# Sizes and pitches of shared on-chip buffers in a gated mix of linear attention and a dense layer

## The chip, the cores and the metric

The kernel runs on one core of one Trainium2 chip. The metric is device time in microseconds (us), the median of three runs. Beside it stands one profiled execution, with the start and duration of every instruction on TensorE (PE; its weight loads are PEld), VectorE (DVE), ScalarE (ACT), GpSimd (POOL) and SyncE (SP, which issues the DMAs).

## The reference

For x of 2048 rows and 640 columns:

```python
g = sigmoid((x * gate_w).sum(-1, keepdims=True))
q, k, v = split(x @ wqkv)                  # 32 heads of 20
phi(t) = concat([softmax(t @ w_phi), softmax(-(t @ w_phi))])   # per head, 40 features
kv = einsum("bhsf,bhsd->bhfd", phi(k), v)  # summed over all rows
z  = einsum("bhsf->bhf", phi(k))
a  = (phi(q) @ kv) / (phi(q) @ z + 1e-6) @ wo
b  = silu(x @ w1) @ w2                     # 1728 hidden columns
out = g * a + (1 - g) * b
```

All of it is float32. The kernel keeps the accuracy by splitting each operand of a matmul into a high part (rounded to float32r) and a low part (the rest), and by three matmuls for one product: high x high, high x low and low x high (PASSES).

## The kernel before, in words

The work has three stages, and TensorE is busy in all of them.

1. **Keys and values** (to about 172 us). The weights for keys and values are prepared in SBUF as two wide tiles, wh (high) and wl (low), of five row chunks with 1282 columns (WC): 640 key columns, 640 value columns and the gate with a column of zeros. For each of 16 tiles of 128 rows, kv_proj (line 470, and line 328 for the first two tiles) multiplies x (stationary, 128 x 128) by wh and wl (moving) in three column cuts: 0 to 500, 500 to 1000, 1000 to 1282. VectorE and ScalarE make the key features from it, v_part (lines 281 to 290) copies the values with high and low part into one of three value tiles vs (line 274), and kv_acc and kv_rest (lines 440 and 451) accumulate kv, with a value row as stationary and the key features as moving operand.

2. **Dense layer** (172 to about 580 us). For four blocks of 512 rows, h_parts (line 518) multiplies a piece of w1 (stationary) by x (moving, 512 elements), ScalarE applies SiLU, the result is split into u, and out_acc (line 706) multiplies a piece of w2 (stationary) by u (moving, 512 elements). One piece costs 15 matmuls at line 518 and 15 at line 706. For the first four pieces of the first block line 535 (h_first) takes the place of line 518. The weights stay in SBUF for all four blocks, in three places that load_f (line 251) chooses by order: the first NPRE = 9 in the pool fq (tiles w), the next ten in the two big buffers (tiles f), the rest in the pool fp (tiles w too). In the last block the fused query weights are made (lines 231 and 246) and the first query tiles run beside the dense work.

3. **Queries and output** (to the end). For eight blocks of 256 rows q_proj (line 429) multiplies x (stationary) by the query weights WQ (moving, 320 elements), VectorE, ScalarE and GpSimd make the features, TensorE transposes them (line 991), multiplies them by kv (line 1128) and by the output weights WO (line 1171; stationary, with oT as moving operand). The last rows of the output weights lie in a tile of their own, wor_s.

The order of work around the change is set in three ways: inside `with inorder(...)` the listed engines run in the order of the code (stage 1's start, the last dense block, and stage 3), a planner orders the rest, and SP issues all DMAs from one queue.

The change touches how SBUF is laid out. **Two big buffers** (tag "big", line 105) are used one after another for three things each: the first for wh, then the held weights f1, then WO; the second for wl, then f0, then WQ. A big buffer holds 2 x 5 x 642 float32r elements (25680 bytes a partition). As `big` it is seen as five chunks with a high and a low half of 642 elements, of which 640 are used; all high halves come first, then all low halves. As `big_kv` it is seen as five rows of 1282 elements without a gap. **The value tiles** (line 274) have 11 rows of 122 elements (VW): 60 high, 60 low, and two ones. The allocation of the pools pads each tile to a multiple of 32 bytes, and tiles of a pool follow each other, so the size of the big buffers decides where everything behind them begins: the raw tiles, the x slots, the pools fq and fu, and the pools that are opened in turn behind these (ta with the value tiles, then fp, then tb).

Of the kernel before, what the change touches and what calls it, by code (L numbers as in the profile page):

```python
# [9 lines left out]
F32R = mybir.dt.float32r  # L10
# [6 lines left out]
P = 128  # L17
S = 2048
D = 640
# [3 lines left out]
NC = D // P  # L23
# [7 lines left out]
GW = GR * DH  # L31
# [7 lines left out]
KG = -(-H // KH)  # L39
VW = KF + 2  # L40
# [10 lines left out]
EB = 2  # L51
KXB = 1
WC = 2 * D + 2
CUTS = (0, 500, 1000, WC)
RW = 114
NEARLY = 3
# [4 lines left out]
def mix_kernel(ctx: ExitStack, tc: tile.TileContext, xT, wqT, wkc, wkr, wv, bd, bdc, cst, wo, w1, w1r, w2, out):  # L61
# [3 lines left out]
    wp = ctx.enter_context(tc.tile_pool(name="wp", bufs=1))  # L65
# [3 lines left out]
    def opened(name, **kw):  # L69
        open_pools[name] = tc.tile_pool(name=name, bufs=1, **kw)  # L70
        return open_pools[name].__enter__()
# [7 lines left out]
    ta = opened("ta")  # L79
# [18 lines left out]
    def raw(name):  # L98
        return wp.tile([P, D + 2], F32, tag="raw", name=name, bufs=4)
# [2 lines left out]
        return (pool or wp).tile([P, 2, 512], F32R, tag=tag, name=name, bufs=bufs)  # L102

    def big_tile(name):
        return wp.tile([P, 2, NC, D + 2], F32R, tag="big", name=name, bufs=2)

    def big(name):
        return big_tile(name).rearrange("p s c d -> p c s d")

    def big_kv(name):  # L110

        return big_tile(name).rearrange("p s c d -> p (s c d)")[:, : NC * WC].rearrange("p (c w) -> p c w", w=WC)

    def wslot(name, dt=F32):
        return fq.tile([P, 2 * D], dt, tag="w", name=name, bufs=NPRE)

    def split(hi, lo, src, lo_eng="dve"):
        nc.scalar.copy(hi, src)  # L118
        eng = nc.vector if lo_eng == "dve" else nc.gpsimd
        eng.tensor_tensor(lo, src, hi.bitcast(F32), op=ALU.subtract)  # L120
# [130 lines left out]
    held = {}  # L251

    def load_f(n):
        w, f = seq[n]
        k = n - NPRE
        if 0 <= k < 10:
            if k % 5 == 0:
                held[k // 5] = big(f"f{k // 5}")
            t = held[k // 5][:, k % 5, :, :D]
        else:  # L260
            t = wslot(f"w{w}_{f}", F32R).rearrange("p (s d) -> p s d", s=2) if n < NPRE else fp.tile([P, 2, D], F32R, name=f"w{w}_{f}")
        r = raw(f"wr{w}_{f}")
        src = w1[f] if w == 1 else w2[f * P : (f + 1) * P, :]
        nc.sync.dma_start(r[:, :D], src)
        split(t[:, 0, :], t[:, 1, :], r[:, :D], "pool" if n < NPRE else "dve")
        W[w, f] = t

    def kv_cols(t, lo, hi):

        k = next(k for k in range(3) if CUTS[k] <= lo and hi <= CUTS[k + 1])  # L270
        return (kvp1 if t == 1 else kvp)[k][:, lo - CUTS[k] : hi - CUTS[k]]

    VB = 3
    vs = [ta.tile([P, KG, VW], F32R, name=f"v{k}") for k in range(VB)]
    for v in vs:
        nc.vector.tensor_copy(v[:, :, KF:], onesf[:, : KG * 2].rearrange("p (g f) -> p g f", f=2))
        nc.vector.tensor_copy(v[:, KG - 1, :KF], onesf[:, :KF])
# [14 lines left out]
    def flat(name):  # L292
        return ta.tile([P, D + 2], F32, tag="kx", name=name, bufs=KXB)

    warm = ps.tile([P, 512], F32, tag="pwk1", name="warm", bufs=1)
    for k in range(WARM):
# [6 lines left out]
        )  # L303

    WKV = [big_kv("wh"), big_kv("wl")]
    wh, wl = (w[:, :, :D] for w in WKV)
    LAST = D - NG * GW
# [33 lines left out]
    def v_weights(c):  # L341
        r = ta.tile([P, 2 * D], F32, tag="e", name="wvr1", bufs=EB)[:, : D + 2] if c == 1 else flat(f"wvr{c}") if c == 2 else raw(f"wvr{c}")
        nc.sync.dma_start(r, wv[c * P : (c + 1) * P, :])
        split(WKV[0][:, c, D:], WKV[1][:, c, D:], r)

    def values(t):
        return [(t, D, CUTS[2]), (t, CUTS[2], WC)]

    def keys(t):
        return [(t, 0, CUTS[1]), (t, CUTS[1], D)]  # L350

    def share(c, cols, opens=()):
        kv_share(c, [(*p, p in opens) for p in cols])

    with inorder(PE, ACT, DVE, POOL):
# [5 lines left out]
        nc.sync.dma_start(strest[: wkr.shape[0], :], wkr)  # L361
        for lo, hi in ((D, CUTS[2]), (CUTS[2], WC)):
            split(WKV[0][:, 0, lo:hi], WKV[1][:, 0, lo:hi], wv0[:, lo - D : hi - D])
# [12 lines left out]
        for c in range(NC):  # L376
            if c + 1 < NC:
                next(x0)
                v_weights(c + 1)
                nc.sync.dma_start(st0[c + 1], wkc[c + 1])  # L380
            for half in range(2):
                k_split_w(c, half, k_weights(c, half))
            if c == 0:
                share(1, values(0) + values(1))
            elif c < 3:
                share(c - 1, keys(0), keys(0)[:1] if c == 1 else ())
            else:
                share(c - 1, [(0, lo, hi) for lo, hi in zip(CUTS, CUTS[1:])])
        share(NC - 1, [(0, lo, hi) for lo, hi in zip(CUTS, CUTS[1:])])
# [198 lines left out]
    with inorder(ACT, DVE, POOL):  # L588
        for t in range(NT - 1):
# [29 lines left out]
            if t % 2 == 1:  # L619
                load_f(t // 2)  # L620
            if t + 2 == NT:
                for _ in range(4):
                    next(xf0)
                load_f(NPRE - 1)
        t = NT - 1
# [84 lines left out]
    with tc.issue_after(last["silu"].ins):  # L710
        for n in range(NPRE, len(seq)):
            load_f(n)
    r = raw("w1rr")
# [4 lines left out]
    r = raw("w2rr")  # L718
# [12 lines left out]

    def wo_split(c):
        r = wor_raw.pop(c)
        split(WO[:GW, c, 0, :D], WO[:GW, c, 1, :D], r[:GW, :D])

    def stack(dst, src, hi, col, n=GW):

# [149 lines left out]
    def make_kvw():  # L887

        parts = [w.rearrange("p j f -> p (j f)").rearrange("p (i q f) -> p i q f", q=4, f=KD) for w in kvw]
        for h in range(2):  # L890
            nc.gpsimd.memset(parts[h][:, :, 1:3].bitcast(F32), 0.0)  # L891
        pts = []
        for j0, n in ((0, 8), (8, 3)):
            pt = bank(f"pkvt{j0}")
            pts.append((j0, n, pt))
            for j in range(j0, j0 + n):
                w = min(KF, 2 * D - j * KF)
                nc.tensor.transpose(
                    pt[:w, (j - j0) * KD : (j - j0 + 1) * KD], kvb["kvm"][:, j * KF : j * KF + w], ident[:KD, :KD]
                )  # L900
        yield
        for j0, n, pt in pts:
            n = min(n, 2 * NG - j0)
            i0, i1 = j0 // 2, (j0 + n) // 2
            split(
                *(part[:, i0:i1, ::3] for part in parts),
                pt[:GW, : n * KD].rearrange("p (i a f) -> p i a f", a=2, f=KD),
            )
        split(
            *(kvwr[:, h].rearrange("p (k f) -> p k f", f=REST) for h in range(2)),  # L910
            pt[:RC, None, n * KD : n * KD + REST].to_broadcast([RC, KH, REST]),
        )
        yield
# [102 lines left out]
    with inorder(PE, DVE, ACT, POOL):  # L1016
# [3 lines left out]
        load_fused(0)  # L1020
        last_dense(4)
        WQ = big("wq")
        zbc = wslot("zbc")
        nc.sync.dma_start(zbc, kv_d[KF].partition_broadcast(P))

        def fuse(gi):
            return fused(kvb["bd"], WQ[:, :, 0, :], WQ[:, :, 1, :], gi)
# [7 lines left out]
        last_dense(6, fuse(1))  # L1035
        kvl_sum(1)
        WO = big("wo")
        load_fused(3)
        wo_load(0)
        last_dense(7, fuse(2))  # L1040
        wo_split(0)
        load_fused(4)
        wo_load(1)
        wo_load(2)
        last_dense(8, fuse(3))
        wo_split(1)
        wo_split(2)
        load_fused(5)
        wo_load(3)
# [3 lines left out]
        w = make_kvw()  # L1053
        last_dense(9, w)
        w = fuse(4)
# [7 lines left out]
        t = 2 * NP - 4  # L1063
# [395 lines left out]
```

## Time and profile before

| | us |
|---|---|
| median of three runs | 761.03 |
| lowest and highest run | 760.9, 761.24 |
| span of the profiled execution | 759.8 |
| PE busy | 755.0 |
| PEld busy | 664.9 |
| DVE busy | 371.6 |
| ACT busy | 266.4 |
| POOL busy | 264.3 |

The span reaches from the first to the last instruction of the profiled execution; that execution has no other time of its own in the profile. In a row of the groups by line stand line, engine, operation, the tiles (output <- inputs), the shapes, the count after an x, then busy us and the mean ns of one, then the idle time before. In a row of the timeline stand start, length, engine, line, operation, tiles, shape and count. In a row of one tile or line stand the shortest, median and longest duration in ns, and the first and last start. In a row of the waits stand who waited for whom, the us in total, how often, and the longest.

### The profile page before, as it was taken

The numbers are of one execution on the slowest core, as the hardware profiler recorded it, in microseconds if no ns is written. First come the engines' busy times: TensorE is split into PE (matmuls) and PEld (weight loads), VectorE is DVE, ScalarE is ACT, GpSimd is POOL, SyncE is SP. The second block draws the span as 40 slices with busy tenths as digits, with TensorE's granted clock in tenths as the row PEclk, the third lists the DMA queues.
The fourth block names the chain that finished last, engine by engine and source line by source line (L and its number), as shares of the span: only waits on it lengthen the run. The fifth ranks groups of instructions, "written<-read, shape, count | busy, mean of one in ns | idle before, by whom it ended". The sixth has DMA issues, their size and how long they took to land.

```text
span 759.8 us, 10642 instructions
## 1 busy us (share of the span) xinstructions
PE 755.0 (99%) x4249; PEld 664.9 (88%) x4249; DVE 371.6 (49%) x664; ACT 266.4 (35%) x483; POOL 264.3 (35%) x165
## 2 busy tenths in 40 slices
PE   9999999999999999999999999999999999999998
PEld 8888888888888888888888888888999999999998
DVE  4676666676641221112211122134578888787861
ACT  5444444337541311122111222224354443334341
POOL 2388777768000000000000000000356766855551
PEclk9999999999999999999999999999999999999999
DMA  7111111112650220002200014022003332111222
GB/s 254 54 53 53 53 53 53 60 49 83 206 175 1 69 83 1 1 0 72 84 0 1 1 40 154 8 81 85 6 29 127 97 104 70 54 52 43 70 70 91
DMA packets 35259, 50.17 MB, mean 66 GB/s; under 512 B 3541, under 2 KB 22885, under 8 KB 35210
## 3 DMA queue, kind: packets, MB, share of 16 engines
q1 hardware_dynamic: 35210, 49.50, 20.7%
q8 instruction: 33, 0.54, 0.3%
q14 instruction: 16, 0.13, 0.1%
HBM read 38.37 MB, written 11.11 MB: 65 GB/s over the span
## 4 chain that ended last, share of the span: by engine, by line
PE 97%; DVE 1%; DMA 0%; POOL 0%; ACT 0%; issue 0%; SPq 0%; POOLq 0%; DVEq 0%; ACTq 0%
PE acc L706 25%; PE ph L518 23%; PE kvp L470 16%; PE pq L429 9%; PE pa L1171 9%; PE pn L1128 4%; PE kv L440 2%; PE pT L991 2%; PE kvp L535 2%; PE kvp L328 1%; PE kvq L328 1%; PE pwk L317 1%; PE pwq L231 1%; DMA wvr<-wv 0%; POOL eq L840 0%; PE kvp L451 0%
## 5 line engine op out<-in xcount | busy, mean ns | idle before, releaser
L120 DVE TENSOR_TENSOR u<-ph,u 128x512 fp32r<-128x512 f32 x48 | 33.2, 692 | 188.5 <-ACT u L118 188.5
L706 PE MATMUL acc<-u,w 128*128 128x512 f32 x480 | 114.2, 391 | 0.0
L891 POOL MEMSET kvw<- 120x600 f32 x2 | 1.2, 598 | 321.1 <-PE ph L518 321.1
L706 PEld LDWEIGHTS acc<-u,w 128*128 128x128 f32 x480 | 89.7, 188 | 19.2
L518 PE MATMUL ph<-xf,w 128*128 128x512 f32 x420 | 99.7, 390 | 0.0
L521 ACT ACTIVATE ph<-ph 128x512 f32<-128x512 f32 x48 | 27.9, 582 | 192.6 <-PE ph L518 192.6
L518 PEld LDWEIGHTS ph<-xf,w 128*128 128x128 f32 x420 | 78.7, 188 | 16.6
L470 PE MATMUL kvp<-wh,xa 128*128 128x500 f32 (+1 forms) x420 | 93.0, 357 | 0.0
L470 PEld LDWEIGHTS kvp<-wh,xa 128*128 128x128 f32 x420 | 71.4, 188 | 9.9
L1171 PE MATMUL pa<-oT,wo 120*128 120x256 f32 x600 | 76.8, 282 | 0.0
L1171 PEld LDWEIGHTS pa<-oT,wo 120*128 120x128 f32 x600 | 73.7, 188 | 0.0
L706 PE MATMUL acc<-u,f 128*128 128x512 f32 x300 | 73.0, 394 | 0.0
L518 PE MATMUL ph<-xf,f 128*128 128x512 f32 x300 | 72.7, 394 | 0.0
L518 PEld LDWEIGHTS ph<-xf,f 128*128 128x128 f32 x300 | 56.4, 188 | 13.1
L706 PEld LDWEIGHTS acc<-u,f 128*128 128x128 f32 x300 | 56.1, 188 | 12.8
L804 POOL TENSOR_TENSOR ez<-eq,zbc 128x1280 f32<-128x1280 f32 x16 | 48.1, 3005 | 41.3 <-ACT eq L787 41.2
L120 POOL TENSOR_TENSOR ph<-ek,ph 128x1280 fp32r<-128x1280 f32 x16 | 47.4, 2964 | 26.8 <-ACT ph L118 26.8
L429 PE MATMUL pq<-wq,xb 128*128 128x320 f32 x360 | 55.5, 311 | 0.0
L429 PEld LDWEIGHTS pq<-wq,xb 128*128 128x128 f32 x360 | 53.0, 188 | 0.0
L470 PE MATMUL kvp<-wl,xa 128*128 128x500 f32 (+1 forms) x210 | 47.4, 356 | 0.0
L840 POOL TENSOR_TENSOR eq<-eq,sm 128x1280 f32<-128x1280 f32 x16 | 37.9, 2368 | 15.1 <-DVE sm L834 13.9
L498 POOL TENSOR_TENSOR ek<-ek,st 128x1280 f32<-128x1280 f32 x16 | 38.0, 2376 | 9.2 <-issue 6.1
(161 smaller groups left out, 1121.8 us busy)
## 6 DMA issues: line engine op xcount, KB each, us to landing
wr<-w SPq DMA_DIRECT2D x26, 320.0 KB, 3.9
xrf<-xT SPq DMA_DIRECT2D x20, 256.0 KB, 3.8
fb_d<-o SPq DMA_DIRECT2D x20, 256.0 KB, 2.4
y<-fb_d SPq DMA_DIRECT2D x16, 256.0 KB, 2.9
out<-y SPq DMA_DIRECT2D x16, 256.0 KB, 2.1
xra<-xT SPq DMA_DIRECT2D x14, 256.0 KB, 3.1
xrb<-xT SPq DMA_DIRECT2D x12, 256.0 KB, 2.7
wvr<-wv SPq DMA_DIRECT2D x5, 321.0 KB, 5.2
```

The costliest lines, as they stand in the source:

```text
L120: eng.tensor_tensor(lo, src, hi.bitcast(F32), op=ALU.subtract)
L328: nc.tensor.matmul(kv_cols(t, lo, hi), x_of(t)[c][:, hx, :], WKV[hw][:, c, lo:hi], start=(opens and hx == 0 and hw == 0), stop=(c == NC - ...
L429: nc.tensor.matmul(dst, xt[c][:, hx, :], w[:, c, hw, lo : lo + n], start=first, stop=(hx == 1 and c == NC - 1))
L470: nc.tensor.matmul(kv_cols(t, lo, hi), xt[c][:, hx, :], WKV[hw][:, c, lo:hi], start=(n == 0), stop=(n == 3 * NC - 1), skip_group_check=True,)
L498: nc.gpsimd.tensor_tensor(groups(e), groups(e), spread(st[:, 1, :]), op=ALU.mult)
L518: nc.tensor.matmul(ph, lhs, rhs, start=(n == 0), stop=(n == len(todo) - 1))
L521: nc.scalar.activation(hs, ph, AF.Silu)
L706: nc.tensor.matmul(acc[m], lhs, rhs, start=(f == order[0] and n == 0), stop=(f == order[-1] and n == len(todo) - 1))
L804: nc.gpsimd.tensor_tensor(ez, Q[t]["e"], zbc, op=ALU.mult)
L840: nc.gpsimd.tensor_tensor(groups(q["e"]), groups(q["e"]), spread(q["sm"][:, 2 * H : 4 * H]), op=ALU.mult)
L1128: nc.tensor.matmul(pns[u, gp][:GW, a, :], kvw_of(hk, 2 * i + jj)[:w], f[:w, hp, jj * 256 : (jj + 1) * 256], start=(n == 0), stop=(n == 3 * ...
L1171: nc.tensor.matmul(pa[:, a, :], WO[:GW, c, hw, ds] if c < NG else WOR[:, ds], o[:, ho, c, :], start=(k == 0), stop=(k == len(todo) - 1),)
```

## The change

Nothing of what is computed changes. The big buffer becomes a plain row of BIG = 2 x 5 x 640 + 32 = 6432 elements (25728 bytes). Seen as `big`, its chunks now hold high and low half next to each other, 640 elements each, without gaps. Seen as `big_kv`, a row has WS = 1284 elements of which 1282 are used. The value tiles get rows of 128 elements of which 122 are used. The remaining lines follow from that: slices that cut 642 down to 640 fall away, and a slice that ran to the end of a key and value row ends at WC.

```diff
 WC = 2 * D + 2
+WS = WC + 2
+BIG = 2 * NC * D + 32
...
     def big_tile(name):
-        return wp.tile([P, 2, NC, D + 2], F32R, tag="big", name=name, bufs=2)
+        return wp.tile([P, BIG], F32R, tag="big", name=name, bufs=2)
 
     def big(name):
-        return big_tile(name).rearrange("p s c d -> p c s d")
+        return big_tile(name)[:, : 2 * NC * D].rearrange("p (c s d) -> p c s d", c=NC, s=2)
 
     def big_kv(name):
 
-        return big_tile(name).rearrange("p s c d -> p (s c d)")[:, : NC * WC].rearrange("p (c w) -> p c w", w=WC)
+        return big_tile(name)[:, : NC * WS].rearrange("p (c w) -> p c w", w=WS)
...
-            t = held[k // 5][:, k % 5, :, :D]
+            t = held[k // 5][:, k % 5]
...
-    vs = [ta.tile([P, KG, VW], F32R, name=f"v{k}") for k in range(VB)]
+    vs = [ta.tile([P, KG, P], F32R, name=f"v{k}")[:, :, :VW] for k in range(VB)]
...
-        split(WKV[0][:, c, D:], WKV[1][:, c, D:], r)
+        split(WKV[0][:, c, D:WC], WKV[1][:, c, D:WC], r)
...
-        split(WO[:GW, c, 0, :D], WO[:GW, c, 1, :D], r[:GW, :D])
+        split(WO[:GW, c, 0], WO[:GW, c, 1], r[:GW, :D])
```

## Prediction

> **What bounds the kernel now.** I read the head of the page first, then the chain that ended last, then the waits of TensorE.
>
> ```profile
> span 759.8 us, 10642 instructions
> PE 755.0 (99%) x4249; PEld 664.9 (88%) x4249; DVE 371.6 (49%) x664; ACT 266.4 (35%) x483; POOL 264.3 (35%) x165
> PEclk9999999999999999999999999999999999999999
> PE 97%; DVE 1%; DMA 0%; POOL 0%; ACT 0%; issue 0%; SPq 0%; POOLq 0%; DVEq 0%; ACTq 0%
> ```
>
> ```profile
> PE warm L297 <- DVE ones L158: 1.1, 1, 1.1
> PE kvp L328 <- ACT wh L118: 0.2, 1, 0.2
> PE pT L991 <- POOL eq L840: 0.2, 1, 0.2
> ```
>
> TensorE is busy 755.0 of 759.8 us, 97% of the chain lies on it, its clock is granted in full in every slice, and all that it waited for another engine comes to 1.5 us. So the end moves only if matmuls themselves follow each other faster or slower. An edit that shortens work of another engine gives nothing here. The question is therefore the pace of the matmul stream: the time from the start of one matmul to the start of the next. The duration of a single row is longer than that, since matmuls overlap; the timeline shows the pace as the distance between the starts of two blocks, over the matmuls in the block.
>
> The dense part has one shape throughout (128 rows, 128 columns, 512 moving elements), and stationary tiles in three places: w tiles in the pool fq, w tiles in the pool fp, and f tiles, which are the ten weights held in the two big buffers. That makes it a control experiment inside the trace. First fq, then the big buffers, then fp, all from the timeline of TensorE:
>
> ```profile
> 282.75 3.56 PE L518 MATMUL ph<-xf,w 128*128 128x512 f32 x15
> 286.15 3.56 PE L706 MATMUL acc<-u,w 128*128 128x512 f32 x15
> 289.55 3.56 PE L518 MATMUL ph<-xf,w 128*128 128x512 f32 x15
> 292.95 3.56 PE L706 MATMUL acc<-u,w 128*128 128x512 f32 x15
> 296.35 3.59 PE L518 MATMUL ph<-xf,f 128*128 128x512 f32 x15
> ```
>
> ```profile
> 216.14 3.62 PE L518 MATMUL ph<-xf,f 128*128 128x512 f32 x15
> 219.60 3.64 PE L706 MATMUL acc<-u,f 128*128 128x512 f32 x15
> 223.07 3.66 PE L518 MATMUL ph<-xf,f 128*128 128x512 f32 x15
> 226.57 3.66 PE L706 MATMUL acc<-u,f 128*128 128x512 f32 x15
> 230.06 2.46 PE L518 MATMUL ph<-xf,w_r 128*128 128x512 f32 x10
> ```
>
> ```profile
> 342.54 3.60 PE L518 MATMUL ph<-xf,w 128*128 128x512 f32 x15
> 345.97 3.60 PE L706 MATMUL acc<-u,w 128*128 128x512 f32 x15
> 349.41 0.85 PE L518 MATMUL ph<-xf,w 128*128 128x512 f32 x3
> ```
>
> Sixty matmuls from fq take 296.35 - 282.75 = 13.60 us, or 3.40 us a block of 15 (226.7 ns a matmul). Sixty from the big buffers take 230.06 - 216.14 = 13.92 us, or 3.48 us a block (232.0 ns). Thirty from fp take 349.41 - 342.54 = 6.87 us, or 3.435 us a block (229.0 ns). Nothing but the place of the stationary operand differs. The groups by line say the same of all matmuls, with a smaller size:
>
> ```profile
> L706 PE MATMUL acc<-u,w 128*128 128x512 f32 x480 | 114.2, 391 | 0.0
> L518 PE MATMUL ph<-xf,w 128*128 128x512 f32 x420 | 99.7, 390 | 0.0
> L706 PE MATMUL acc<-u,f 128*128 128x512 f32 x300 | 73.0, 394 | 0.0
> L518 PE MATMUL ph<-xf,f 128*128 128x512 f32 x300 | 72.7, 394 | 0.0
> ```
>
> The mean of one is 3 and 4 ns longer with f than with w.
>
> **Where the operands start.** In the program of before, the first big buffer begins at byte 17792 of a partition (278 x 64) and the second at 43488 (679.5 x 64). A held weight k with half s lies k x 2568 + s x 12840 bytes further, so its start moves by 8 and 40 bytes against a multiple of 64: 17 of the 20 rows start off one. The tiles in fq, x and u start at 192 modulo 512, those in fp at 128 modulo 512, all on multiples of 64. Thus the best pace belongs to stationary and moving tiles at the same offset, the middle one to tiles 64 bytes apart, the worst to rows off the multiples of 64. After the change a big buffer has 25728 bytes (402 x 64) in place of 25680, padded to 25696, and everything behind the two moves by 64 bytes: x, u and fq to 256 modulo 512, fp to 192. The second big buffer then starts at 43520, at 0 modulo 512, and the first still at 384; each held row is a multiple of 2560 = 5 x 512 further. So all f rows lie 256 or 128 bytes from x and u, modulo 512.
>
> **The change part by part.** No instruction, DMA, wait or queue position is added or removed; the order of work, the shapes and the bytes moved stay. What changes is addresses.
>
> *Held weights (load_f).* They feed 300 + 300 matmuls, 40 blocks of 15. At the pace of fp the gain is 40 x (3.48 - 3.435) = 1.8 us, at the pace of fq 40 x (3.48 - 3.40) = 3.2 us; by the means of one, 300 x 3 + 300 x 4 ns = 2.1 us. The new distances are multiples of 128, as fq's distance of 0 is, and fp's 64 is not; so I take a value nearer to fq: 3.41 us a block, 40 x 0.07 = **2.8 us**. Bounds: 0, if the place of the buffer and not its phase is slow, and 3.2. If the stream is faster, what feeds it is early enough: DVE and ACT are busy 49% and 35%, and of the three waits above none lies in this stretch. [...]
>
> *Key and value weights (big_kv).* They are the moving operand of 630 matmuls, N = 500 and 282. The row pitch goes from 5128 (8 off a multiple of 64) to 5136 (16 off), so rows start at 0, 16, 32, 48 and 0 where they started at 0, 8, 16, 24 and 32, and the column cuts at 500 and 1000 elements add 16 and 32 as before. Only a part is on a multiple of 64 in either layout.
>
> ```profile
> L470 PE MATMUL kvp<-wh,xa 128*128 128x500 f32 x280 | 70.5, 389 | 0.0
> L470 PE MATMUL kvp<-wl,xa 128*128 128x500 f32 x140 | 36.1, 387 | 0.0
> L470 PE MATMUL kvp<-wh,xa 128*128 128x282 f32 x140 | 22.9, 293 | 0.0
> L470 PE MATMUL kvp<-wl,xa 128*128 128x282 f32 x70 | 11.3, 292 | 0.0
> ```
>
> wh lies in the first buffer and wl in the second, 32 bytes off in phase, and they differ by 2 ns with 500 elements and by 1 with 282. That bounds the part: 630 x 2 ns = 1.3 us either way. The phases become other ones, not better ones; I take 0. [...]
>
> *Query weights (WQ) and output weights (WO).* Both come to lie on multiples of 512 from their buffer's start.
>
> ```profile
> L429 PE MATMUL pq<-wq,xb x360: 304/308/397, 582.0 to 714.7; 128*128 128x320 f32 x180
> L429 PE MATMUL pq<-wq,xf x120: 304/308/313, 532.9 to 566.4; 128*128 128x320 f32 x120
> ```
>
> ```profile
> L1171 PE MATMUL pa<-oT,wo x600: 276/281/367, 595.1 to 756.1; 120*128 120x256 f32 x150
> L1171 PE MATMUL pa<-oT,wor_s x40: 280/282/283, 596.9 to 756.2; 120*128 120x256 f32 x40
> ```
>
> These columns are the shortest, the median and the longest duration. For the output there is a control: wor_s lies in a pool of its own on a multiple of 64, and its median of 282 is no better than the 281 of the unaligned WO. So I take 0 there; bounds 600 x 5 ns = 3.0 us of gain if all went to the shortest, 600 x 1 ns = 0.6 us of loss. For the queries there is no control; I take 0, with 480 matmuls x 4 ns = 1.9 us either way.
>
> *Value tiles (vs).* The stationary rows of kv_acc and kv_rest get a pitch of 512 bytes in place of 488.
>
> ```profile
> L440 PE MATMUL kv<-ph,v x160: 271/273/279, 41.7 to 185.7; 128*121 128x240 f32 x160
> ```
>
> 160 matmuls, with 2 ns from the median to the shortest and 6 to the longest: a gain of 0.3 us at most, a loss of 1.0 at most; I take 0, since the median is by the lower end already. [...]
>
> The sum is -2.8 us: the span goes from 759.8 to 757.0 us. The median of the three runs is 761.03, 1.2 us above the span, and no edit touches that part, so the time is 761.0 - 2.8 = **758.2 us**.
>
> **The rivals.** *Nothing changes.* The f tiles may be slow for a reason other than their phase, such as the region in which the buffer lies. For it speaks that fp, on a multiple of 64, is 2.3 ns slower than fq: alignment alone doesn't give the best pace. Against it speaks that a moving operand from the same two buffers shows a dependence on phase too (wh against wl). The time is 761.0. [...]
>
> *Everything speeds up.* Besides the 2.8 us, WQ and WO go to their shortest durations: 2.8 + 1.9 + 3.0 = 7.7 us, 753.3 us; half of the second part gives 755.8. The row of wor_s speaks against it.
>
> *Slower: the shift of 64 bytes.* All buffers behind the two big ones move by 64 bytes, x, u and the w tiles among them. If it is the offset itself that sets the pace and not the distance between the two operands, the blocks from fq and fp lose what they have. The first pieces (h_first) count with the 480 and 420 above.
>
> ```profile
> L535 PE MATMUL kvp<-xf,w x60: 387/389/404, 172.4 to 188.4; 128*128 128x512 f32 x60
> ```
>
> These are 960 matmuls with w tiles, 64 blocks; the nine tiles in fq serve 540 of them (36 blocks), those in fp 420 (28 blocks). At the worst pace seen, 3.48, that is 36 x 0.08 + 28 x 0.045 = 4.1 us, and with f unchanged the time is 765.1. It decides from 64 blocks x 0.044 us on, where it eats the 2.8. For it: the three paces are known at one set of offsets only. Against it: all these tiles move together, so their distances stay, and only f, WQ, WO and the key and value weights move against them.
>
> *The change doesn't do what it says.* The addresses follow from the sizes, and this can't be otherwise for f, WQ and WO; for the key and value weights it holds in part only, which is in the sum.
>
> **How the numbers follow.** Forecast (758.2, own range 756.5 to 759.6): 0.60. Everything speeds up (755.8 and below to 753.3): 0.14. Nothing changes (761.0, give or take 1): 0.17. Slower by the shift (762.6 to 765.1): 0.09. A measurement of this kernel tells about 0.2% (1.5 us) from no change. Below 759.5 lie nearly all of the forecast's case and the second: 0.70. Within 759.5 to 762.5 lie the third and what is left of the others: 0.21. Slower: 0.09. The range reaches from 755.0, which takes in half of the second case, to 761.4, which takes in most of the third; the bounds of the unknown costs (1.3 and 1.9 us) lie within it.
>
> **What would show it.** In the profile of the changed kernel the blocks ph<-xf,f and acc<-u,f should start 3.40 to 3.44 us apart, and their means of one fall from 394 to 390 or 391; the w blocks should keep 3.40 and 3.435. The kvp rows should stay at 387 to 389, pq at a median of 308, pa at 281 or 282, kv at 273. The waits of TensorE should stay near 1.5 us in all. I am wrong if f stays at 3.48 (place, not phase), if the w blocks move (offset, not distance), or if kvp, pq or pa move by more than 2 ns a matmul: these hold 1710 matmuls, and 2 ns on all of them is 3.4 us, as much as the whole forecast.

## The result, and the profile after

The median went from 761.09 us (20 runs, 760.81 to 761.59) to 759.75 us (20 runs, 759.27 to 760.33): 1.34 us less, a ratio of 0.9982 with a 95% interval of 0.9975 to 0.9989. The sign of the forecast held and the time lies in its range of 755.0 to 761.4, though just outside the 756.5 to 759.6 that the forecast gave its main case; the size was about half of the 2.8 us forecast.

The head of the page after, and the waits of TensorE (who waited for whom, us in total, times, longest):

```profile
span 758.3 us, 10642 instructions
PE 753.5 (99%) x4249; PEld 664.2 (88%) x4249; DVE 371.3 (49%) x664; ACT 266.3 (35%) x483; POOL 264.4 (35%) x165
```

```profile
PE warm L299 <- DVE ones L160: 1.1, 1, 1.1
PE kvp L330 <- ACT wh L120: 0.3, 1, 0.3
```

The span and TensorE's busy time both fell by 1.5 us; the other engines and the number of instructions stayed, and no wait came up. So the gain lies in the pace of the matmuls, as it had to. The groups by line of after (count, then busy us and the mean ns of one; every line number is two higher than before):

```profile
L708 PE MATMUL acc<-u,w 128*128 128x512 f32 x480 | 114.1, 391 | 0.0
L520 PE MATMUL ph<-xf,w 128*128 128x512 f32 x420 | 99.8, 390 | 0.0
L1173 PE MATMUL pa<-oT,wo 120*128 120x256 f32 x600 | 76.6, 280 | 0.0
L708 PE MATMUL acc<-u,f 128*128 128x512 f32 x300 | 72.3, 392 | 0.0
L520 PE MATMUL ph<-xf,f 128*128 128x512 f32 x300 | 72.3, 392 | 0.0
L472 PE MATMUL kvp<-wh,xa 128*128 128x500 f32 x280 | 70.5, 389 | 0.0
L431 PE MATMUL pq<-wq,xb 128*128 128x320 f32 x360 | 55.3, 310 | 0.0
L472 PE MATMUL kvp<-wl,xa 128*128 128x500 f32 x140 | 36.0, 387 | 0.0
L442 PE MATMUL kv<-ph,v 128*121 128x240 f32 x160 | 22.0, 273 | 0.0
```

Two of them in the profile before, which the prediction did not show in this view:

```profile
L1171 PE MATMUL pa<-oT,wo 120*128 120x256 f32 x600 | 76.8, 282 | 0.0
L429 PE MATMUL pq<-wq,xb 128*128 128x320 f32 x360 | 55.5, 311 | 0.0
```

The held weights f give 73.0 + 72.7 - 72.3 - 72.3 = 1.1 us, WO 0.2 and WQ 0.2. The w groups, the key and value groups and the value tiles move by 0.1 at most. The largest rise is that of pn (line 1130), from 35.4 to 35.6. The mean of f fell only half of the way from 394 to the 390 of w. The timeline of after shows why (start, length, then the block; the pace is the distance between starts, and the last row is there for its start; w_r is the small last piece of the weights):

```profile
215.89 3.65 PE L520 MATMUL ph<-xf,f 128*128 128x512 f32 x15
219.38 3.57 PE L708 MATMUL acc<-u,f 128*128 128x512 f32 x15
222.79 3.65 PE L520 MATMUL ph<-xf,f 128*128 128x512 f32 x15
226.27 3.56 PE L708 MATMUL acc<-u,f 128*128 128x512 f32 x15
229.67 0.62 PE L520 MATMUL ph<-xf,w_r 128*128 128x512 f32 x2
```

Here line 520 reads f1, which lies in the first big buffer, and line 708 reads f0, in the second. The f0 blocks now take 222.79 - 219.38 = 3.41 and 3.40 us, the best pace. The f1 blocks take 3.49 and 3.48; before, the four f blocks of this stretch took 3.46 to 3.50. All rows of both buffers now start on multiples of 64. One buffer has the best pace, the other stayed slow.

### The profile page after: what moved, and what is told of

It reads as the page before. It is cut to its first block, busy times and chain, and to the rows that moved or that the text cites. A ratio compares the mean times of both kernels' runs of the same rounds, so it can differ in the third digit from the quotient of the medians.

```text
span 758.3 us, 10642 instructions
## 1 busy us (share of the span) xinstructions
PE 753.5 (99%) x4249; PEld 664.2 (88%) x4249; DVE 371.3 (49%) x664; ACT 266.3 (35%) x483; POOL 264.4 (35%) x165
## 4 chain that ended last, share of the span: by engine, by line
PE 97%; DVE 1%; DMA 1%; SPq 0%; ACT 0%; POOL 0%; issue 0%; POOLq 0%; DVEq 0%; ACTq 0%
PE acc L708 25%; PE ph L520 23%; PE kvp L472 16%; PE pq L431 9%; PE pa L1173 9%; PE pn L1130 4%; PE kv L442 2%; PE pT L993 2%; PE kvp L537 2%; PE kvp L330 1%; PE kvq L330 1%; PE pwq L233 1%; PE pwk L319 1%; DMA wvr<-wv 1%; POOL eq L842 0%; PE kvp L453 0%
## 5 line engine op out<-in xcount | busy, mean ns | idle before, releaser
L708 PE MATMUL acc<-u,w 128*128 128x512 f32 x480 | 114.1, 391 | 0.0
L520 PE MATMUL ph<-xf,w 128*128 128x512 f32 x420 | 99.8, 390 | 0.0
L708 PE MATMUL acc<-u,f 128*128 128x512 f32 x300 | 72.3, 392 | 0.0
L520 PE MATMUL ph<-xf,f 128*128 128x512 f32 x300 | 72.3, 392 | 0.0
```

The source lines that it names most:

```text
L520: nc.tensor.matmul(ph, lhs, rhs, start=(n == 0), stop=(n == len(todo) - 1))
L708: nc.tensor.matmul(acc[m], lhs, rhs, start=(f == order[0] and n == 0), stop=(f == order[-1] and n == len(todo) - 1))
```

## The experiments

The theory after the result: **the pace of a matmul with 512 moving elements depends on the distance of its moving and its stationary operand modulo 256 bytes** (the start of the moving one less the start of the stationary one). f0 lies at distance 0 from x and u after the change, f1 at 128. The rivals: multiples of 64 are enough and the first buffer's region is slow (A); the start of the stationary row itself modulo 128 counts (B); the start of all operands modulo 256 counts, not their distance (C). All experiments are edits of the changed kernel. The view `big` gets a second argument where a diff uses it, by which its elements start `at` elements (4 bytes each) into the buffer:

```diff
-    def big(name):
-        return big_tile(name)[:, : 2 * NC * D].rearrange(...)
+    def big(name, at=0):
+        return big_tile(name)[:, at : at + 2 * NC * D].rearrange(...)
```

**Moving f1 alone.**

```diff
-                held[k // 5] = big(f"f{k // 5}")
+                held[k // 5] = big(f"f{k // 5}", (0, 32)[k // 5])
```

> The held weights f1 in the first big buffer start 128 bytes later; nothing else moves. Theory (the pace of a 512-element matmul is set by the distance of its moving and its stationary operand modulo 256): f1 goes from distance 128 to 0, its 20 blocks of 15 go from 3.48 or 3.49 us to 3.40, and the time falls by 1.5 to 1.7 us below the changed kernel, to about 758.1 us. Rival A (multiples of 64 are enough, and f1 is slow because of the region where the first buffer lies): f1 stays at 3.48 or 3.49, the time at 759.7.

Measured: 758.33 us, ratio to before 0.9962 (0.995 to 0.9975). The timeline of this kernel:

```profile
215.68 3.56 PE L520 MATMUL ph<-xf,f 128*128 128x512 f32 x15
219.08 3.56 PE L708 MATMUL acc<-u,f 128*128 128x512 f32 x15
222.48 3.56 PE L520 MATMUL ph<-xf,f 128*128 128x512 f32 x15
225.88 3.56 PE L708 MATMUL acc<-u,f 128*128 128x512 f32 x15
229.28 1.08 PE L520 MATMUL ph<-xf,w_r 128*128 128x512 f32 x4
```

All four blocks take 3.40 us. 128 bytes within the same buffer bring the other half of the gain, though f1 started on multiples of 64 already and stays in its region: rival A falls.

**Moving f0 alone.** The same edit with (32, 0).

> The held weights f0 in the second big buffer start 128 bytes later; f1 stays as in the changed kernel. Theory (distance modulo 256): f0 goes from distance 0 to 128, its blocks from 3.40 to 3.48 or 3.49 us, and the time rises by 1.4 to 1.7 us above the changed kernel, to about 761.2 us, where it was before the change. Rival A (multiples of 64 are enough, the region does the rest): f0 stays at 3.40 and the time at 759.7.

Measured: 761.63 us, ratio 1.0007 (0.9998 to 1.0016): the change is undone in full. The timeline:

```profile
215.94 3.65 PE L520 MATMUL ph<-xf,f 128*128 128x512 f32 x15
219.43 3.65 PE L708 MATMUL acc<-u,f 128*128 128x512 f32 x15
222.91 3.64 PE L520 MATMUL ph<-xf,f 128*128 128x512 f32 x15
226.39 3.65 PE L708 MATMUL acc<-u,f 128*128 128x512 f32 x15
229.88 0.40 PE L520 MATMUL ph<-xf,w_r 128*128 128x512 f32 x1
```

Every row still starts on a multiple of 128 bytes, and every block takes 3.48 or 3.49 us.

**Both by 64 bytes.** The same edit with (16, 16).

> Both f0 and f1 start 64 bytes later, so all rows stay on multiples of 64. Theory (distance modulo 256): f0 goes to distance 192, where the few blocks of before took about 3.49 us, f1 to distance 64, the one of the pool fp, 3.435 us. So f0 slows by about 1.8 us in all, f1 gains about 1.0, and the time is about 760.5 us. Rival A (multiples of 64 are enough): neither moves, 759.7 us. Rival B (it is the start of the stationary row itself modulo 128 that counts, 0 good and 64 bad): both at 64, both at fp's 3.435, f0 loses 0.7 and f1 gains 1.0, 759.4 us.

Measured: 760.78 us, ratio 0.9996 (0.9987 to 1.0005). The timeline:

```profile
215.99 3.61 PE L520 MATMUL ph<-xf,f 128*128 128x512 f32 x15
219.44 3.66 PE L708 MATMUL acc<-u,f 128*128 128x512 f32 x15
222.94 3.66 PE L520 MATMUL ph<-xf,f 128*128 128x512 f32 x15
226.44 3.65 PE L708 MATMUL acc<-u,f 128*128 128x512 f32 x15
229.93 0.39 PE L520 MATMUL ph<-xf,w_r 128*128 128x512 f32 x1
```

The f0 blocks (line 708, distance 192) take 3.50 and 3.49 us, as expected from the distance; rival B wanted 3.435. The first f1 block (line 520, distance 64) takes 3.45, the second 3.50. The same distance has two paces here, which the theory doesn't explain (more at the end). All of these rows start on multiples of 64.

**Everything by 128 bytes.**

```diff
-    ones = cp.tile([P, P], F32R, name="ones")
+    ones = cp.tile([P, P + 32], F32R, name="ones")[:, :P]
```

> A constant tile ahead of all buffers grows by 128 bytes, so every buffer of the changed kernel moves by 128 and no distance between two buffers changes. Theory (distance): f0 stays at 3.40, f1 at 3.48 or 3.49, the w blocks at 3.40 and 3.435, the time at 759.7 us. Rival C (the start itself modulo 256 counts): f0 and f1 change roles (f1 at 0, f0 at 128), and the w blocks of both pools change their pace, the 36 blocks from fq by up to 0.08 us each, 2.9 us.

Measured: 759.66 us, ratio 0.998 (0.9971 to 0.9989), the time of the changed kernel. The timeline:

```profile
218.82 3.57 PE L708 MATMUL acc<-u,f 128*128 128x512 f32 x15
222.23 3.65 PE L520 MATMUL ph<-xf,f 128*128 128x512 f32 x15
225.71 3.56 PE L708 MATMUL acc<-u,f 128*128 128x512 f32 x15
229.11 1.08 PE L520 MATMUL ph<-xf,w_r 128*128 128x512 f32 x4
```

f0 at 3.41 and 3.40 and f1 at 3.48, though f1 now starts at 0 modulo 256 and f0 at 128. Rival C falls: what counts is the distance, as far as a common shift by 128 bytes can show it.

**Small distances.** Three kernels place f0 and f1 some bytes to either side of distance 0: the same edit with (4, 28) for 16 bytes, (2, 30) for 8 and (8, 24) for 32.

> The held weights lie 16 bytes from distance 0: f0 starts 16 bytes later than in the changed kernel, f1 112 bytes later; all their rows are multiples of 16 and none is one of 64. Theory (distance modulo 256, 0 being the one good value): the few blocks of before at such distances took 17 to 20 ns over the 213 of 512 elements where distance 0 takes 13.7, so 600 matmuls lose about 4 to 5 ns each, 2.4 to 3 us over f1_plus128: 760.7 to 761.3 us. [...]

> As f_off16, with 8 bytes in place of 16: f0 at distance 248 modulo 256, f1 at 8, all rows at an odd multiple of 8. By the blocks of before at these two distances (17.8 and 20.0 ns over the 213 of 512 elements, where distance 0 takes 13.7): 300 x 4.1 + 300 x 6.3 ns = 3.1 us over f1_plus128, 761.4 us. Theory D (a row has to start on a multiple of 16 bytes, and be within 16 of distance 0): the same loss. Rival (near distance 0 anything is fast): 758.3 us.

> As f_off16, with 32 bytes: f0 at distance 224, f1 at 32, all rows on multiples of 32. By the blocks of before (16.6 and 20.0 ns): 300 x 2.9 + 300 x 6.3 ns = 2.8 us over f1_plus128, 761.1 us. [...]

Measured: 758.18 us for 16 bytes (ratio 0.9963, 0.995 to 0.9975), 761.32 for 8 (1.0004, 0.9995 to 1.0013), 763.41 for 32 (1.0031, 1.0019 to 1.0044). The groups by line of the three, in this order:

```profile
L708 PE MATMUL acc<-u,f 128*128 128x512 f32 x300 | 71.7, 390 | 0.0
L520 PE MATMUL ph<-xf,f 128*128 128x512 f32 x300 | 71.3, 389 | 0.0
```

```profile
L708 PE MATMUL acc<-u,f 128*128 128x512 f32 x300 | 73.0, 395 | 0.0
L520 PE MATMUL ph<-xf,f 128*128 128x512 f32 x300 | 73.0, 395 | 0.0
```

```profile
L708 PE MATMUL acc<-u,w 128*128 128x512 f32 x480 | 115.0, 394 | 0.0
L520 PE MATMUL ph<-xf,w 128*128 128x512 f32 x420 | 100.4, 392 | 0.0
L708 PE MATMUL acc<-u,f 128*128 128x512 f32 x300 | 73.4, 396 | 0.0
L520 PE MATMUL ph<-xf,f 128*128 128x512 f32 x300 | 73.2, 395 | 0.0
```

With 16 bytes the loss that was expected didn't come; with 8 bytes it came as expected (3.0 us over f1_plus128), and with 32 it was 5.1 us over f1_plus128 where 2.8 were expected. That a start on a multiple of 16 bytes is enough would fit 16 (758.18 us) and 8 (761.32); but 32 is a multiple of 16 too and is the slowest of all (763.41), so that doesn't decide the pace either. The 213 ns for 512 elements from which two of the expectations count their paces is shown by no run; the trace of before shows 226.7 ns a matmul at distance 0, and the sums use differences alone (4.1, 6.3 and 2.9 ns). Against the 390 and 389 ns of f in f1_plus128 the means of one rose by 0 with 16 bytes, by 5 and 6 ns with 8, and by 6 with 32.

Neither multiples of 64 nor of 16 are enough, and a start off 64 may be as good as any: in these runs distance 0 and 16 to either side are fast (3.40 us a block), 8 (3.50 at 8, 3.46 at 248), 32 (means of one of 396 and 395 ns), 128 (3.48 or 3.49) and 192 (3.49 or 3.50) are slow, and 64 is between (3.435 from fp, 3.45 and 3.50 in both_plus64). The set of good places is not known from this. Theory D, in the expectation for 8 bytes (a multiple of 16, within 16 of distance 0), fits these three kernels, but the trace of before speaks against it. There the f block of line 518 at 296.35 has ten matmuls at distance 216, whose rows start at an odd multiple of 8, and five at 176; the next block starts at 299.77, so it took 3.42 us, close to the best. And with 32 bytes the w groups got slower as well (115.0 and 100.4 us against 114.1 and 99.8 in the changed kernel), though none of their operands moved.

**The pool fp to distance 0.** On top of the edit of f1:

```diff
-        kvwr = fu.tile([RC, 2, GW], F32R, name="kvwr")
+        kvwr = fu.tile([RC, 2 * GW + 16], F32R, name="kvwr")[:, : 2 * GW].rearrange("p (h f) -> p h f", h=2)
```

> As f1_plus128, and 64 bytes more in the pool fu, so that fp (and what is opened behind it: the value tiles, the key features, oT, wor_s) moves by 64 bytes against x and u. Theory (distance modulo 256): the w tiles of fp go from distance 64 to 0, their 28 blocks from 3.435 to 3.40 us, a gain of 28 x 0.035 = 1.0 us over f1_plus128's 758.3, to about 757.4 us; w_r, which lies in fp as well, may add 0.1. Rival (the pool fp is slower for another reason, such as its region): no gain, 758.3 us.

Measured: 757.9 us, ratio 0.9959 (0.9947 to 0.9972). The groups by line, first of f1_plus128, then of this kernel:

```profile
L708 PE MATMUL acc<-u,w 128*128 128x512 f32 x480 | 114.3, 392 | 0.0
L520 PE MATMUL ph<-xf,w 128*128 128x512 f32 x420 | 99.8, 390 | 0.0
L1173 PE MATMUL pa<-oT,wo 120*128 120x256 f32 x600 | 76.7, 281 | 0.0
```

```profile
L708 PE MATMUL acc<-u,w 128*128 128x512 f32 x480 | 113.6, 390 | 0.0
L520 PE MATMUL ph<-xf,w 128*128 128x512 f32 x420 | 99.4, 389 | 0.0
L1173 PE MATMUL pa<-oT,wo 120*128 120x256 f32 x600 | 77.7, 283 | 0.0
```

The w groups gain 0.7 + 0.4 = 1.1 us, what the theory gave. The output matmuls give 1.0 back; their moving operand oT lies in the pool tb, which is opened where fp was and moved with it. The times of the two kernels can't be told apart.

**WO to distance 0 from oT.** On top of the last kernel, `WO = big("wo", 32)`.

> As f1_fp, and WO starts 128 bytes later in the first big buffer, so that WO and oT go from distance 128 to 0. In f1_fp the 600 output matmuls took 120.3 ns each against 118.5 to 118.8 elsewhere. Theory (distance modulo 256 holds for 256 elements too): they fall to 116 to 118 ns, 1.4 to 2.6 us less than f1_fp's 757.9, about 756 us. Rival (it holds for 512 elements alone, and f1_fp's loss came from elsewhere): 757.9 us.

Measured: 758.17 us, ratio 0.9963 (0.9949 to 0.9976); the output group:

```profile
L1173 PE MATMUL pa<-oT,wo 120*128 120x256 f32 x600 | 78.0, 284 | 0.0
```

78.0 against 77.7: distance 0 brings these matmuls nothing, and the 756 us that the theory gave did not come. The theory is one of 512 moving elements; what sets the pace of those with 256 stays open.

**Padding between the two big buffers, and both together.**

```diff
-        return wp.tile([P, BIG], F32R, tag="big", name=name, bufs=2)
+        first = name in ("wh", "f1", "wo")
+        return wp.tile([P, BIG + 32 * first], F32R, tag=f"big{int(first)}", name=name, bufs=1)[:, :BIG]
```

> The first big buffer alone grows by 128 bytes, so the second one, x, u and all behind move by 128 against it: f1 at distance 0 like f0, and also wh (moving operand of the key and value matmuls) and WO at another distance. Theory for f1 as in f1_plus128: 758.3 us from f1 alone. For wh, worked out from the mean pace at each distance in the traces before and after: 1.5 ns less on 420 matmuls, 0.6 us, so about 757.7 us. Rival (the distance counts only where the moving operand has 512 elements): wh doesn't move and the time is 758.3.

> pad_between and the 64 bytes in fu together: f0, f1, both w pools, WQ and WO all lie at distance 0 from what they meet, and wh keeps pad_between's place. Theory: f1_fp_wo and the 0.4 us that wh gained in pad_between, about 755.6 us, the fastest of all. Rival (the gains are not independent): no better than pad_between, 758.1 us.

Measured: 758.14 us (0.9962, 0.9949 to 0.9974) and 758.15 us (0.9964, 0.9951 to 0.9976). For pad_between the group of wh:

```profile
L473 PE MATMUL kvp<-wh,xa 128*128 128x500 f32 x280 | 70.2, 388 | 0.0
```

It gains 0.3 us against 70.5, half of what was expected. In pad_fp the output group loses again, 1.4 us against the 76.7 of f1_plus128, so the gains did not add up to the 755.6 us expected:

```profile
L1174 PE MATMUL pa<-oT,wo 120*128 120x256 f32 x600 | 78.1, 284 | 0.0
```

So the best that was found lies at 757.9 to 758.3 us, 3 us or 0.4% below before and some 1.5 us below the changed kernel; f1_plus128 reaches it with one number.

**Undoing the pitches.**

```diff
-WS = WC + 2
+WS = WC
...
-    vs = [ta.tile([P, KG, P], F32R, name=f"v{k}")[:, :, :VW] for k in range(VB)]
+    vs = [ta.tile([P, KG, VW], F32R, name=f"v{k}") for k in range(VB)]
```

> The changed kernel with two of its parts undone: rows of 1282 elements for the key and value weights, of 122 for the value tiles; the buffers stay where they are. Theory (the whole gain is f0's new distance): 759.7 us, as the changed kernel, within 0.3. Rival (the pitches bring part of the gain): 760 us or more.

Measured: 760.35 us, ratio 0.999 (0.9981 to 0.9999), 0.6 us above the changed kernel, outside the 0.3 expected and where the rival put it; the two intervals overlap, so the times alone don't settle it. The trace shows where:

```profile
L472 PE MATMUL kvp<-wl,xa 128*128 128x500 f32 x140 | 36.5, 390 | 0.0
```

36.5 against 36.0 in the changed kernel and 36.1 before. With the rows' old pitch the new place of the second buffer (its start moves by 32 bytes and that of x by 64) cost wl 0.4 us (36.5 against 36.1); the new pitch makes up for it (36.0).

## Why the prediction was right in sign and half in size

- **The bound** held: only the pace of the matmuls moved, with waits of 1.4 us in all. The copies and subtractions that write the held rows did not matter: their medians are 728 and 824 ns after, 728 and 826 before.
- **Held weights:** forecast 2.8 us, measured 1.1 in the rows of f. The step that failed is the sentence "The new distances are multiples of 128, as fq's distance of 0 is, and fp's 64 is not; so I take a value nearer to fq". It took a period of 128 from distances of 0 and 64 alone. For the multiples of 128 seen here the period is 256: f0 at distance 0 got fq's 3.40, f1 at distance 128 kept 3.48 (after, f0_plus128), and 128 bytes more gave f1 the rest (f1_plus128). With half of the blocks at 3.41 and half at 3.48 the same working gives 20 x 0.07 = 1.4 us. A smaller fault is that 3.48 stood for every f block, "the worst to rows off the multiples of 64": four of the twenty at line 518 took 3.42 or 3.43 us already, with rows off 64 (296.35 to 299.77 is one). With both buffers at distance 0 (f1_plus128) the whole gain was 2.8 us, so the size forecast was that of the better layout.
- **Key and value weights:** 0 was right, and for another reason than "other phases, not better ones": the shift of the second buffer and the new pitch cancel within 0.1 us (big_only).
- **Query and output weights, value tiles:** 0.2 us each for the first two, inside the bounds, and 0 for the tiles. wor_s as a control for WO was read well, and it says more after: its mean fell from 282 to 280 ns, as WO's did, though it keeps its distance to oT. So WO's 0.2 us is not shown to come from WO's new rows.
- **Nothing changes** was half true: f1 stayed as slow as it was (3.48 and 3.49 us a block), though not for its region (3.40 in f1_plus128, within the same buffer). The prediction's argument against the region, wh against wl, could not tell: these lie in different buffers. In f1_plus128 and f0_plus128 nothing but a stationary tile moved, and 300 matmuls changed their pace by 0.08 us a block of 15, 5 ns each: the place of a stationary tile does matter here.
- **Everything speeds up** and **the shift of 64 bytes** did not come: WQ and WO hardly moved, and the w groups stayed at 114.1 and 99.8. The change moved x, u and both w pools together by 64 bytes, and all_plus128 by 128; neither common shift cost the w blocks anything.
- That the change does what it says was true of the addresses; that multiples of 64 are what the chip rewards was not.

## What to carry to other kernels

Where TensorE sets the end, compare the distance between the starts of blocks of equal matmuls whose operands lie in different buffers: a few ns a matmul may point to where the operands lie. Then look at the distance of the two operands of one matmul, not at the alignment of each; here, with 512 float32r elements, 0 modulo 256 bytes was among the best (226.7 ns a matmul) and 128 and 192 cost 5 to 7 ns. It did not carry over to the output matmuls with 256 elements (78.0 us at distance 0, 77.7 at 128). Try a placement and read the pace, since the whole set of good distances is not known. Padding moves all that lies behind it, so look for the group that pays: in f1_fp the w groups gained 1.1 us and the output matmuls gave 1.0 back.

## What was not expected of the hardware

One distance can have two paces. In the kernel with 32 bytes the w blocks of fp, none of whose operands moved, follow the slow f blocks at the slow pace:

```profile
343.26 3.67 PE L520 MATMUL ph<-xf,w 128*128 128x512 f32 x15
346.76 3.66 PE L708 MATMUL acc<-u,w 128*128 128x512 f32 x15
350.26 2.03 PE L520 MATMUL ph<-xf,w 128*128 128x512 f32 x8
```

They take 3.50 us where the same blocks took 3.435 before and 3.43 in the changed kernel (341.81 to 345.24 to 348.67), and the w groups together lost 0.9 + 0.6 us against the changed kernel (115.0 and 100.4). In the last dense block of the same kernel, where these pieces come behind the weights of fq, they are back at 3.45 and 3.44 us (539.38 to 542.83 and 550.64 to 554.08). So the same tiles at the same addresses run at both paces, and what ran before seems to decide.

What it is about the work before stays open, for it isn't its pace alone. In the kernel with 8 bytes two f blocks take 3.50 us (330.00 to 333.50 to 337.00), and the w block behind them takes 3.43 (to 340.43); the w groups of that kernel stay at 114.2 and 99.8 us. In both_plus64 the second f1 block, at distance 64, takes 3.50 behind a block at distance 192, but the first one takes 3.45 behind such a block too (212.50 to 215.99). No run was made to settle it.

Nor is it settled why 16 bytes are as good as 0 while 8 and 32 are not, and why the output matmuls lost 1.0 to 1.4 us, against f1_plus128, in each of the three kernels in which oT moved by 64 bytes more. There WO lies at distance 128 or 0 from oT, elsewhere at 64 or 192 (76.3 to 76.7 us in the kernels with the new layout); but wor_s, which kept its distance, lost too (280 to 282 or 283 ns), so the distance is not shown to be the cause. The runs also don't tell whether a matmul's own moving operand counts or the one that is read while its weights are loaded (after, PEld is busy 664.2 and PE 753.5 of 758.3 us, so loads lie beside matmuls), since x and u start alike.
